# Seven products of quarters in place of the last expert's second product

## The chip, the core and the metric

The program runs on one core of a Trainium2 chip. The metric is the time of one execution on the device, in microseconds (us). The engines are TensorE (PE; PEld is its weight load), VectorE (DVE), ScalarE (ACT), GpSimd (POOL) and SyncE (SP), which here issues the transfers (DMAs).

## What is computed

Three layers follow one another, in float32: attention with a forgetting bias (2 x 8 heads, 576 tokens each), then a mixture of 8 experts on the 1152 tokens, then a bilinear layer.

```python
P = np.exp(logits)                 # then 8 rounds of row and column normalisation
for e in range(8):
    h = np.maximum(x @ w1[e], 0.0)         # 1152 x 512 by 512 x 1024: the first product
    ye = h @ w2[e]                         # 1152 x 1024 by 1024 x 512: the second product
    out += P[:, e:e + 1] * ye
a = out @ w_a
b = out @ w_b                              # 512 x 1536 each
return (a * b) @ w_out                     # 1536 x 512
```

## The kernel before

**Number format.** Every operand is split into a high and a low float16 half. A float32 product is three matmuls: high by high, high by low, low by high. A split is two instructions: ScalarE rounds the value to the high half (a plain copy that casts, or `hi_of`, L295, with a scale), and VectorE writes value minus high (`lo_of`, L309, for weights and for the last tokens; plain subtractions elsewhere).

**Tiles.** The 1152 tokens are 9 tiles of 128, in the order of the list `ORDER`. `xt` holds their transposed inputs, `ht` the hidden values (8 row blocks of 128 by 1152 tokens, two halves), `acc` the weighted sum over the experts. PSUM has eight banks, `mb0` to `mb2` and `yb0` to `yb4`.

**Stages.** Expert 0 runs beside the attention. Expert 1 makes its first product plainly (`h_plain`). Experts 2 to 7 make theirs by a Winograd form (`h_seven`): both operands are cut into quarters (tokens in two halves of 576, so `CN` is 288 columns) and seven products of quarters, each 6 matmuls of 288 columns, replace eight. Partial sums stay in PSUM; `dve_add` (L1713) and `act_copy` (L1717) move them between banks, and `out` (L1708, L1709) applies the maximum with zero and splits the result into `ht`. The sums of the inputs are made once (`x_sums`, L1622, tile `sx`), those of the weights for each expert (`w_sums`, L1656). The second product is plain in every expert: `y_tile` runs 24 matmuls of 512 columns for each tile (`y_part`, L1308 to L1310), and L1754 adds the scaled result to `acc`. In the last expert `xm_split` scales, splits and transposes each finished tile back into `xt`, and `x2_sums` (L1799) forms the sums that the bilinear layer's own seven products need. In that layer `ab_plain` (L1886) handles one tile plainly, `ab_seven` (L1924) eight tiles; `out_stage` (L2014) has matmuls of 256 columns.

**Conversions.** The bilinear layer's weights arrive as pairs of 32-bit words of float64 and are turned into float16 halves by `m2_prep`, 18 pieces, each a chain of some 16 VectorE instructions (L1525 to L1533, L1549, two of L309), a few on ScalarE and one on GpSimd. `m2_out` stores each piece in DRAM, and `m2_in` fetches it again. `M2N` says how many pairs of pieces each of the experts 1 to 7 carries beside its matmuls: none, then 4, 2, 4, 2, 4 and 2 pieces in experts 2 to 7. A piece may begin only after its expert's first product has written its first result (the key `hold`).

**Order.** Up to the first expert the order is written out by hand. From there on a planner (`Graph.schedule`) lays out all operations: each has an engine, or a choice between two, a cost in ns, the keys that it reads and writes, and a rank. The planner always takes the operation that can start first, and by rank among those within 60 ns. The result is a fixed order for each engine, and each engine runs its own list in order.

## Time and profile before

| what | us |
|---|---|
| median of 3 runs | 1011.77 (1010.45 to 1011.91) |
| the profiled execution, its own time | 1010.49 |
| its span, first to last instruction | 1008.8 |

The granted clock of TensorE is 1.0 of full speed (2.4 GHz) throughout. The profile is of one execution. Its span leaves out 1.7 us ahead of the first and behind the last instruction. A window is a stretch of the span; a group is all instructions with the same line, engine and operands. A busy TensorE is not one at its peak, since a matmul's record (0.38 us for 512 columns) overlaps those of its neighbours; the distance between starts, or a stretch divided by its count, tells more.

### The profile page before, as it was taken

The page shows a single profiled execution, that of the slowest core. Times are in us where ns is not written, and L with a number is a line of the kernel's source. Part 1 is how long each engine was busy: PE and PEld are TensorE (multiplying, and loading weights), DVE is VectorE, ACT ScalarE, POOL GpSimd, SP SyncE. Part 2 cuts the span into 40 slices and gives each one's busy share as a digit, 9 for nine tenths or more (in the row PEclk, how much of TensorE's full clock was granted, in tenths as well). Part 3 has the DMA queues.
Part 4 walks back from the last instruction along what each step waited for, and adds up shares of the span by engine and source line. Part 5 has one row for each costly group of instructions (what it writes and reads, how often), then busy time and mean ns, then how long its engine had stood idle before and what let it go on. Part 6 is the DMA issues. An engine that isn't in the chain of part 4 may idle for free.

```text
span 1008.8 us, 18859 instructions
## 1 busy us (share of the span) xinstructions
PE 989.8 (98%) x7534; PEld 629.5 (62%) x7534; DVE 774.8 (77%) x1661; ACT 530.9 (53%) x1009; POOL 99.7 (10%) x150
## 2 busy tenths in 40 slices
PE   6799999999999999999999999999999999999998
PEld 5677767665467547646744764674476464555777
DVE  4899996689858998875898896689888886667402
ACT  5798753563356438626644762663464454545220
POOL 3364563000000000000000000000000000000000
PEclk9999999999999999999999999999999999999999
DMA  9986999320241254224125414313446432313202
GB/s 235 208 167 123 172 168 171 97 94 1 76 134 43 84 209 167 84 97 154 44 104 188 167 69 137 130 43 116 177 171 244 97 85 84 126 44 124 84 21 74
DMA packets 152008, 121.38 MB, mean 120 GB/s; under 512 B 113360, under 2 KB 127696, under 8 KB 147312
## 3 DMA queue, kind: packets, MB, share of 16 engines
q1 hardware_dynamic: 147008, 117.78, 41.1%
q10 hardware_dynamic: 4912, 2.40, 1.0%
q8 instruction: 59, 0.97, 0.4%
q14 instruction: 29, 0.24, 0.1%
HBM read 79.26 MB, written 21.23 MB: 100 GB/s over the span
## 4 chain that ended last, share of the span: by engine, by line
PE 91%; DVE 3%; DMA 2%; ACT 1%; SPq 1%; issue 1%; POOL 1%; ACTq 0%; DVEq 0%; POOLq 0%
PE yb L1310 11%; PE yb L1309 11%; PE yb L1308 11%; PE yb L1700 4%; PE yb L1698 4%; PE yb L1699 4%; PE mb L1698 3%; PE mb L1699 3%; PE mb L1700 3%; PE yb L1925 2%; PE yb L1924 2%; PE yb L1926 2%; PE mb L1265 2%; PE mb L1267 2%; PE mb L1266 2%; PE mb L1925 2%
## 5 line engine op out<-in xcount | busy, mean ns | idle before, releaser
L1308 PE MATMUL yb<-wun,ht 128*128 128x512 f16 x504 | 191.0, 379 | 0.0
L1309 PE MATMUL yb<-wun,ht 128*128 128x512 f16 x504 | 191.0, 379 | 0.0
L1310 PE MATMUL yb<-wun,ht 128*128 128x512 f16 x504 | 191.0, 379 | 0.0
L1310 PEld LDWEIGHTS <-ht 128*128 128x128 f16 x504 | 49.3, 98 | 59.5
L1308 PEld LDWEIGHTS <-ht 128*128 128x128 f16 x504 | 49.4, 98 | 58.8
L1309 PEld LDWEIGHTS <-ht 128*128 128x128 f16 x504 | 49.3, 98 | 58.8
L1698 PE MATMUL yb<-sx,wun 128*128 128x288 f16 x288 | 82.4, 286 | 0.0
L1699 PE MATMUL yb<-sx,wun 128*128 128x288 f16 x288 | 82.4, 286 | 0.0
L1700 PE MATMUL yb<-sx,wun 128*128 128x288 f16 x288 | 82.4, 286 | 0.0
L309 DVE SCALAR_TENSOR_TENSOR wun<-stage,sc,wun 128x1024 f16<-128x1024 f32 (+1 forms) x70 | 75.9, 1108 | 7.7 <-ACT wun L295 7.5
L1754 DVE SCALAR_TENSOR_TENSOR acc<-yb,pe,acc 128x512 f32<-128x512 f32 x63 | 47.3, 750 | 44.5 <-PE yb L1310 43.6
L1699 PEld LDWEIGHTS <-wun 128*128 128x128 f16 x672 | 65.8, 98 | 17.5 <-issue 0.3
L1698 PEld LDWEIGHTS <-wun 128*128 128x128 f16 x672 | 65.8, 98 | 17.1
L1700 PEld LDWEIGHTS <-wun 128*128 128x128 f16 x672 | 65.8, 98 | 16.6
L295 ACT ACTIVATE wun<-stage,sc 128x1024 f16<-128x1024 f32 (+1 forms) x60 | 60.8, 1045 | 21.1 <-PE yb L1310 14.3
L292 ACT ACTIVATE jk<-stage 128x1024 f16<-128x1024 f32 x52 | 54.8, 1054 | 31.6 <-DMA stage<-in_moe_w_dram 30.9
L295 ACT ACTIVATE wun<-h,sc 128x1024 f16<-128x1024 f32 x36 | 41.1, 1144 | 27.1 <-issue 17.3
L1698 PE MATMUL mb<-xt,wun 128*128 128x288 f16 x192 | 54.9, 286 | 0.2 <-ACT yb L1717 0.2
L1700 PE MATMUL mb<-xt,wun 128*128 128x288 f16 x192 | 54.9, 286 | 0.0
L1699 PE MATMUL mb<-xt,wun 128*128 128x288 f16 x192 | 54.9, 286 | 0.0
L1708 ACT ACTIVATE ht<-yb 128x288 f16<-128x288 f32 x96 | 38.9, 408 | 26.5 <-PE yb L1700 26.3
L1288 PE MATMUL mb<-xt,wun 128*128 128x128 f16 x288 | 51.4, 222 | 0.6 <-DVE acc L1333 0.6
(507 smaller groups left out, 2553.4 us busy)
## 6 DMA issues: line engine op xcount, KB each, us to landing
stage<-in_moe_w_dram SPq DMA_DIRECT2D x26, 1024.0 KB, 5.1
md<-wun SPq DMA_DIRECT2D x18, 1024.0 KB, 3.9
wun<-md SPq DMA_DIRECT2D x12, 1024.0 KB, 4.8
mr<-in_moe_w_a_dram SPq DMA_DIRECT2D x12, 512.0 KB, 6.1
mr<-in_moe_w_b_dram SPq DMA_DIRECT2D x12, 512.0 KB, 3.5
mr<-in_moe_w_out_dram SPq DMA_DIRECT2D x12, 512.0 KB, 4.6
stage<-md SPq DMA_DIRECT2D x5, 1024.0 KB, 4.7
stage<-in_moe_w_dram SPq DMA_DIRECT2D x19, 256.0 KB, 4.1
```

What stands on the lines that cost most here:

```text
L292: nc.scalar.activation(out, src, AF.Square, accum_out=dst)
L295: nc.scalar.activation(hi, src, AF.Copy, scale=scale)
L309: eng.scalar_tensor_tensor(out=lo, in0=src, scalar=scale, in1=hi, op0=ALU.mult, op1=ALU.subtract)
L1288: nc.tensor.matmul(p, lhsT=wh, rhs=xh, start=(c == 0), stop=False)
L1308: nc.tensor.matmul(pp, lhsT=hh, rhs=wh, start=(f == 0), stop=False)
L1309: nc.tensor.matmul(pp, lhsT=hh, rhs=wl, start=False, stop=False)
L1310: nc.tensor.matmul(pp, lhsT=hl, rhs=wh, start=False, stop=(f == KF - 1))
L1698: nc.tensor.matmul(p, lhsT=wh, rhs=xh, start=first and ch == 0, stop=False, skip_group_check=True)
L1699: nc.tensor.matmul(p, lhsT=wh, rhs=xl, start=False, stop=False, skip_group_check=True)
L1700: nc.tensor.matmul(p, lhsT=wl, rhs=xh, start=False, stop=ch == 1, skip_group_check=True)
L1754: g.add("DVE", 663, lambda t=t, z=z: nc.vector.scalar_tensor_tensor(out=acc[:, t], in0=yb[z], scalar=pe[:, t, e:e + 1], in1=acc[:, t], op0 ...
L1925: nc.tensor.matmul(p, lhsT=wh, rhs=xl, start=False, stop=False, skip_group_check=True)
```

## The change

For the last expert (`YSEVEN`) the second product of eight of the nine tiles is made by seven products of quarters (`y_seven`): the 1024 hidden rows and the 512 output columns are halved, and the tokens are taken in pairs of tiles (`ORDER[kk]` and `ORDER[5 + kk]`). Matmuls have 256 columns. The ninth tile, `ORDER[4]`, is made plainly from four blocks (`rest_mm`), with 256 columns too.

The hidden values of that expert are no longer split by `out`. ScalarE writes them, scaled by 0.25, as float32 into `r`, a larger tile in the place of `ts0` and `ts1`. `h_parts`, called after each of the four rounds of `h_seven`, splits the quarters and forms their sums: four sums of 128x512 on GpSimd, eight low halves on VectorE, eight high halves on ScalarE, four of which may go to GpSimd. `w2_sums` forms and splits seven weight quarters: 4 subtractions, 7 high and 7 low halves of 128x1024, where `w_prep` had 4 and 4. The results lie in the new tile `wx`, in `units` 2 and 3 and in `sx`.

So that the quarters are whole tiles, `ORDER[4]` is divided between the two halves. `x_sums` reads `xt` through two pieces, and `x_turn` then moves the second half of `xt` by four transfers. In experts 2 to 6 the ninth tile's hidden values now lie in two places, and `r_copy` collects them into `wx` by two transfers per expert (256 KB each, pieces of 128 bytes); `y_tile` reads there for tile 4. `x2_sums` may put its sums on GpSimd for three of four groups. `M2N` gives experts 2 to 7 now 4, 4, 4, 4, 2 and 0 pieces.

```diff
+        big["wx"] = bp.tile([128, 2, 2, 1024], F16, name="wx")
         for i in range(2):
-            big["ts", i] = bp.tile([128, 1024], F32, name=f"ts{i}")
+            big["ts", i] = big["r"][:, i * 1024:(i + 1) * 1024]
...
+        def f():
+            nc.vector.tensor_scalar(pe[:, :, e], pe[:, :, e], inv1[e], inv2[e], op0=ALU.mult, op1=ALU.mult)
+            if e in YSEVEN:
+                nc.vector.tensor_scalar(pe[:, :, e], pe[:, :, e], 1.0 / HSC, None, op0=ALU.mult)
...
+            def X(z, r, t, c=c):
+                v = lambda c0, c1: xt[:, z, 2 * r + c, c0:c1]
+                return (lambda: (v(640, 1152), v(512 + 64, 640))) if t else (lambda: v(0, HT))
+
...
+    def x_turn():
+
+        rk = 203
+        xk = [("xt", t) for t in range(NTL)]
+        m = lambda: stage[2].bitcast(F16).rearrange("p (a t) -> p a t", a=8)
+        v = lambda c0, c1: xt[:, :, :, c0:c1].rearrange("p z c t -> p (z c) t")
+        n = lambda: h0[1].rearrange("p z f t -> p (z f t)")[:, 0:512].rearrange("p (a t) -> p a t", a=8)
+        mk = [("st", 2, c) for c in range(4)]
+        g.add("SP", 900, lambda: nc.sync.dma_start(out=m(), in_=v(640, 1152)), r=xk, w=mk, rank=rk)
+        g.add("SP", 200, lambda: nc.sync.dma_start(out=n(), in_=v(HT, 640)), r=xk, w=h0k[1], rank=rk)
+        g.add("SP", 900, lambda: nc.sync.dma_start(out=v(HT, 1088), in_=m()), r=mk, w=xk, rank=rk)
+        g.add("SP", 200, lambda: nc.sync.dma_start(out=v(1088, 1152), in_=n()), r=h0k[1], w=xk, rank=rk)
...
+    def h_parts(j):
+
+        R = lambda q: big["r"][:, q * HT:q * HT + 512]
+        k = lambda q: [("r", q, c) for c in range(2)]
+        rest = lambda: big["r"].rearrange("p (a b t) -> p a b t", a=2, b=2)[:, :, :, 512:HT]
+        home = lambda z: h_rest(z).rearrange("p (a f) (b t) -> p a f b t", a=2, b=2)[:, :, j]
+        rk = -4.5
+        g.add("ACT", 360, lambda: nc.scalar.activation(home(0), rest(), AF.Copy), r=rkeys, w=[("HR", 0, j)], rank=rk)
+        g.add("DVE", 420, lambda: nc.vector.tensor_tensor(out=home(1), in0=rest(), in1=home(0), op=ALU.subtract), r=rkeys + [("HR", 0, j)], w=[("HR", 1, j)], rank=rk)
+
+        def split(i, q, pool):
+            hi, lo = (lambda z=z: h_op(i, z)[:, j] for z in range(2))
+            g.add(("ACT", "POOL"), (620, 700), (lambda: nc.scalar.activation(hi(), R(q), AF.Copy), lambda: nc.gpsimd.tensor_copy(hi(), R(q))),
+                  r=k(q), w=[("H", i, 0, j)], rank=rk)
+            g.add("DVE", 690, lambda: nc.vector.tensor_tensor(out=lo(), in0=R(q), in1=hi(), op=ALU.subtract), r=k(q) + [("H", i, 0, j)], w=[("H", i, 1, j)], rank=rk)
+
+        def tt(o, a, b, op):
+            g.add("POOL", 1300, lambda: nc.gpsimd.tensor_tensor(out=R(o), in0=R(a), in1=R(b), op=op), r=k(a) + k(b), w=k(o), rank=rk)
+
+        split(1, 0, False)
+        split(2, 2, False)
+        split(4, 3, False)
+        tt(3, 1, 3, ALU.add)
+        split(5, 3, True)
+        tt(1, 0, 1, ALU.subtract)
+        split(7, 1, True)
+        tt(0, 3, 0, ALU.subtract)
+        split(6, 0, True)
+        tt(2, 2, 0, ALU.subtract)
+        split(3, 2, True)
...
+            v = [(lambda z=z: w2_at(e, i)(z)) for z in range(2)]
+            wk = w2_keys(e, i)
+            g.add("ACT", 1144, lambda: hi_of(v[0](), src(), sx), r=keys + [("ws", 2, e)], w=wk[0], rank=rank)
+            g.add("DVE", 1290, lambda: lo_of(nc.vector, v[1](), src(), sx, v[0]()), r=keys + [("ws", 2, e)] + wk[0], w=wk[1], rank=rank)
+
+        split(0, b11, k11)
+        sub(b11, b12, b11, k12, k11)
+        sub(b12, b22, b12, k22, k12)
+        split(3, b11, k11)
+        sub(b11, b22, b11, k22, k11)
+        split(4, b12, k12)
+        split(5, b11, k11)
+        split(1, b21, k21)
+        sub(b11, b21, b11, k21, k11)
+        split(2, b22, k22)
+        split(6, b11, k11)
...
+    def y_seven(e, hook):
+
+        wof = {1: 0, 2: 1, 3: 2, 4: 6, 5: 3, 6: 5, 7: 4}
+        G, gk = [lambda: yb[1], lambda: mb[0]], [[("yG", n, h) for h in range(2)] for n in range(2)]
+        Y, yk = [lambda: mb[2], lambda: mb[1]], [[("yY", n)] for n in range(2)]
+        links = [([("yb", 1)], gk[0]), (mbk(2), yk[0]), (mbk(0), gk[1]), (mbk(1), yk[1])]
...
+        def prod(i, kk, bank, bk, first, more=()):
+            wv, wk = w2_at(e, wof[i]), w2_keys(e, wof[i])
+            for j in range(4):
+                def mm(j=j):
+                    p = bank()
+                    hh, hl = (h_op(i, z)[:, j, kk * 128:(kk + 1) * 128] for z in range(2))
+                    wh, wl = (wv(z)[:, j] for z in range(2))
+                    nc.tensor.matmul(p, lhsT=hh, rhs=wh, start=first and j == 0, stop=False, skip_group_check=True)
+                    nc.tensor.matmul(p, lhsT=hh, rhs=wl, start=False, stop=False, skip_group_check=True)
+                    nc.tensor.matmul(p, lhsT=hl, rhs=wh, start=False, stop=j == 3, skip_group_check=True)
+
+                g.add("PE", 3 * 108, mm, r=[("H", i, z, j) for z in range(2)] + wk[0] + wk[1], w=bk + (list(more) if j == 0 else []), rank=frank())
+
+        def add(t, h, bank, bk, n=256):
+            v = lambda: acc[:, t, h * 256:h * 256 + n]
+            g.add("DVE", 440 if n == 256 else 750, lambda: nc.vector.scalar_tensor_tensor(
+                out=v(), in0=bank(), scalar=pe[:, t, e:e + 1], in1=v(), op0=ALU.mult, op1=ALU.add), r=bk + [("pe", e)], w=[("acc", t)], rank=-5)
+            g.add("-", LAG, lambda: None, w=bk)
+
+        half = lambda f, h: (lambda: f()[:, h * 256:(h + 1) * 256])
+        rest = []
+        for kk in range(5):
+            n = kk % 2
+            ta, tb = (ORDER[kk], ORDER[5 + kk]) if kk < 4 else (0, 0)
+            X, F, U = half(G[n], 0), half(G[n], 1), half(Y[n], 0)
+            xk, fk, uk = gk[n][0:1], gk[n][1:2], yk[n]
+            if kk < 4:
+                prod(1, kk, X, xk, True, fk)
+                prod(5, kk, F, fk, False)
+                g.add("ACT", 390, lambda U=U, X=X: nc.scalar.activation(U(), X(), AF.Copy), r=xk, w=uk, rank=-6)
+                g.add("-", LAG, lambda: None, w=xk + uk)
+                add(tb, 1, F, fk)
+                prod(2, kk, X, xk, False)
+                add(ta, 0, X, xk)
+            for f in rest:
+                f()
+            rest = []
+            if kk < 4:
+                prod(6, kk, U, uk, False)
+                add(ta, 1, U, uk)
+                prod(3, kk, F, fk, False)
+                add(ta, 1, F, fk)
+                prod(7, kk, U, uk, False)
+                add(tb, 1, U, uk)
+
+                def end(kk=kk, U=U, uk=uk, ta=ta, tb=tb):
+                    prod(4, kk, U, uk, False)
+                    add(tb, 0, U, uk)
+                    hook(ta)
+                    hook(tb)
+                    if kk:
+                        x2_sums(kk - 1)
+
+                rest.append(end)
...
+        def rest_mm(kh, wi, h, first):
+            wv, wk = w2_at(e, wi), w2_keys(e, wi)
+
+            def mm():
+                p = yb[0][:, h * 256:(h + 1) * 256]
+                for j in range(4):
+                    hh, hl = (h_rest(z)[:, 4 * kh + j] for z in range(2))
+                    wh, wl = (wv(z)[:, j] for z in range(2))
+                    nc.tensor.matmul(p, lhsT=hh, rhs=wh, start=first and j == 0, stop=False, skip_group_check=True)
+                    nc.tensor.matmul(p, lhsT=hh, rhs=wl, start=False, stop=False, skip_group_check=True)
+                    nc.tensor.matmul(p, lhsT=hl, rhs=wh, start=False, stop=j == 3, skip_group_check=True)
...
+        rest_mm(0, 0, 0, True)
+        add(t, 1, half(lambda: yb[0], 0), [("yb", 0)])
+        rest_mm(1, 2, 1, False)
+        rest_mm(0, 3, 1, False)
+        rest_mm(1, 1, 0, False)
+        add(t, 0, lambda: yb[0], [("yb", 0)], 512)
+        hook(t)
+        x2_sums(3)
...
+        seven = e in YSEVEN
+
         def out(src, bk, f, s_, c):
+            if seven:
+                q = 2 * (f // 4) + s_
+                g.add("ACT", 172 + CN / 1.2, lambda: nc.scalar.activation(big["r"][:, q * HT + c * CN:q * HT + (c + 1) * CN], src(), AF.Relu, scale=HSC),
+                      r=bk, w=[("r", q, c)], rank=-5)
+                return
...
+            if seven:
+                h_parts(j)
+
+    r_home = lambda: big["wx"].rearrange("p i z f -> p (i z f)")[:, 0:2048].rearrange("p (z f t) -> p z f t", z=2, f=8)
+
+    def r_copy():
+        for i, c0 in enumerate((512, 1088)):
+            g.add("SP", 400, lambda i=i, c0=c0: nc.sync.dma_start(
+                out=r_home()[:, :, :, i * 64:(i + 1) * 64].rearrange("p z f t -> p (z f) t"),
+                in_=big["ht"][:, :, :, c0:c0 + 64].rearrange("p z f t -> p (z f) t")),
+                r=[x for z in range(2) for f in range(KF) for x in hk(z, f, c0, c0 + 64)], w=[("wx", 0, y) for y in range(2)], rank=-4)
...
+        if e > 1 and p > 4:
+            dst, dkey = h_cols(p * 128 - 64, p * 128 + 64)
+        elif e > 1 and p == 4:
+            dst, dkey = (lambda z, f: r_home()[:, z, f]), (lambda z, f: [("wx", 0, y) for y in range(2)])
...
+            both = YSEVEN and not lo and kk < 3
+            g.add(("DVE", "POOL") if both else "DVE", (400, 750) if both else 400, tuple(fn) if both else fn[0], r=r, w=w, rank=rk)
...
-M2N = (0, 2, 1, 2, 1, 2, 1)
+M2N = (0, 2, 2, 2, 2, 1, 0)
+YSEVEN = (7,)
+HSC = 0.25
```

## Rows read from the trace of the kernel before

**Rows 1.** Page: the span, and busy time and share of each engine.

```profile
span 1008.8 us, 18859 instructions
...
PE 989.8 (98%) x7534; PEld 629.5 (62%) x7534; DVE 774.8 (77%) x1661; ACT 530.9 (53%) x1009; POOL 99.7 (10%) x150
```

**Rows 2.** Page, part 4: the chain that ended last, share of the span.

```profile
PE 91%; DVE 3%; DMA 2%; ACT 1%; SPq 1%; issue 1%; POOL 1%; ACTq 0%; DVEq 0%; POOLq 0%
```

**Rows 3.** Windows: stretch, its length, busy us (instructions) per engine, PEclk, DMA, GB/s.

```profile
379.40:466.46 87.06, 87.06 (x547) 53.42 (x546) 69.27 (x127) 48.30 (x86) 1.84 (x4) 1.00 0.31 109
466.46:554.24 87.78, 87.78 (x553) 54.01 (x552) 76.89 (x145) 47.30 (x89) 2.33 (x6) 1.00 0.37 132
683.50:730.12 46.62, 46.62 (x219) 21.13 (x216) 42.42 (x70) 18.20 (x25) 1.62 (x4) 1.00 0.43 158
730.12:771.28 41.16, 41.16 (x338) 32.88 (x336) 34.45 (x70) 26.01 (x56) 0.61 (x1) 1.00 0.45 158
771.28:817.90 46.62, 46.62 (x219) 21.13 (x216) 40.55 (x122) 18.09 (x37) 0.57 (x1) 1.00 0.49 150
817.90:825.94 8.04, 8.04 (x146) 8.04 (x144) 7.22 (x23) 5.08 (x14) 0.00 (x0) 1.00 0.71 196
944.07:974.20 30.13, 30.13 (x278) 27.01 (x276) 8.94 (x15) 6.51 (x14) 0.00 (x0) 1.00 0.24 88
```

**Rows 4.** Waits of TensorE from 560 to 575 us.

```profile
PE mb L1698 <- ACT yb L1717: 0.2, 1, 0.2
```

**Rows 5.** Groups by form, VectorE, expert 4: line, operation, count, busy us, mean ns, idle before.

```profile
L309 DVE SCALAR_TENSOR_TENSOR wun<-stage,sc,wun 128x1024 f16<-128x1024 f32 x6 | 7.7, 1280 | 1.0 <-ACT wun L295 1.0
...
L1754 DVE SCALAR_TENSOR_TENSOR acc<-yb,pe,acc 128x512 f32<-128x512 f32 x9 | 6.8, 751 | 3.4 <-PE yb L1310 3.1
...
L1533 DVE SCALAR_TENSOR_TENSOR h<-h,h 128x1024 int32<-128x1024 int32 x4 | 4.9, 1215 | 0.0
L1713 DVE TENSOR_TENSOR yb<-yb,sw 128x288 f32<-128x288 f32 x8 | 3.7, 462 | 1.3 <-PE yb L1700 1.3
...
L1549 DVE TENSOR_TENSOR h<-h,h 128x256 f32<-128x256 f32 x8 | 3.3, 418 | 0.0
...
L1526 DVE TENSOR_SCALAR h<-h,clampi 128x1024 f32<-128x1024 f32 x4 | 3.2, 807 | 0.0
L1528 DVE TENSOR_SCALAR h<-h 128x1024 int32<-128x1024 int32 x4 | 2.8, 695 | 0.0
...
L1656 DVE TENSOR_TENSOR ts<-stage,ts 128x1024 f32<-128x1024 f32 x2 | 2.4, 1220 | 0.0
```

**Rows 6.** Groups by form, VectorE, 818 to 944 us.

```profile
L1941 DVE TENSOR_TENSOR ht<-h,ht 128x512 f16<-128x512 f32 x10 | 6.6, 683 | 0.0
```

**Rows 7.** Groups by form, GpSimd, 97 to 170 us.

```profile
L977 POOL TENSOR_TENSOR pt<-p,pt 128x512 f16<-128x512 f32 x14 | 16.2, 1158 | 7.1 <-DMA raw<-pt 2.1 <-ACT pt L974 2.1 <-DVE pt L973 1.6
L974 POOL CAST pt<-p 128x512 f16<-128x512 f32 x9 | 5.9, 656 | 8.6 <-ACT p L1035 7.0 <-issue 1.6
```

**Rows 8.** Timeline, GpSimd and VectorE: start, length, instruction.

```profile
69.77 1.90 POOL L915 TENSOR_TENSOR pt<-p,pt 128x512 f16<-128x512 f32 x1 [4.53 <-ACT pt L912]
...
69.97 0.68 DVE L914 TENSOR_TENSOR pt<-p,pt 128x512 f16<-128x512 f32 x1
...
156.36 1.16 POOL L977 TENSOR_TENSOR pt<-p,pt 128x512 f16<-128x512 f32 x1 [2.11 <-DMA raw<-pt]
...
156.89 1.17 DVE L976 TENSOR_TENSOR pt<-p,pt 128x512 f16<-128x512 f32 x1 [0.57 <-ACT pt L974]
```

**Rows 9.** Timeline, VectorE and TensorE inside the last first product.

```profile
746.57 0.46 DVE L1713 TENSOR_TENSOR yb<-yb,sw 128x288 f32<-128x288 f32 x1
...
747.76 0.29 PE L1698 MATMUL yb<-sx,wun 128*128 128x288 f16 x1
```

**Rows 10.** Page, part 6: DMA issues, count, size, us to landing.

```profile
wun<-md SPq DMA_DIRECT2D x12, 1024.0 KB, 4.8
...
stage<-in_moe_w_dram SPq DMA_DIRECT2D x19, 256.0 KB, 4.1
```

More of the change, by code (lines that the diff above doesn't have):

```diff
@@ new lines, in w2_sums, with sub, split @@
+    def w2_sums(e, rank):
+        z0, z1 = wst[2, e]
+        sx = ws[2, e]
+        qk = [("q2", z, h) for z in (z0, z1) for h in range(2)]
+        stk = [("st", z, c) for z in (z0, z1) for c in range(4)]
+        g.add("-", 0, lambda: None, w=qk + stk)
+        b11, b12, b21, b22 = ((lambda z=z, h=h: stage[z].rearrange("p (c f) -> p c f", c=4)[:, :, h * 256:(h + 1) * 256]) for z in (z0, z1) for h in range(2))
+        k11, k12, k21, k22 = ([x] for x in qk)
+        def sub(o, a, b, r, w):
+            g.add("DVE", 1280, lambda: nc.vector.tensor_tensor(out=o(), in0=a(), in1=b(), op=ALU.subtract), r=r, w=w, rank=rank)
+        def split(i, src, keys):
+            v = [(lambda z=z: w2_at(e, i)(z)) for z in range(2)]
[13 more added lines that the diff above has]
+        split(6, b11, k11)
+        g.add("-", 0, lambda: None, w=qk + stk)
@@ L2131, in forgetting_attention_moe_bilinear_kernel @@
         else:
+            if e in YSEVEN:
+                h_link()
+                r_link()
             h_seven(e)
-        w_prep(2, e, (2, 3), prank())()
+            if e in YSEVEN:
+                r_link()
+            else:
+                r_copy()
+        if e in YSEVEN:
+            w_prep(2, e, (None, None), prank())
+            w2_sums(e, prank())
+        else:
+            w_prep(2, e, (2, 3), prank())()
         if e == 1:
             x_sums()
+            x_turn()
         if not last:
```

81 lines of the change are left out of this document (63 added, 18 removed).

## The prediction

> **What bounds the kernel now.** I read the page first: TensorE is busy 98% of the span [rows 1], and the chain that ended last lies 91% on it [rows 2]. Since a busy TensorE can still run thinly, the windows come next: each matmul has one weight load, so a stretch divided by PEld's count is the distance between starts. In the last expert's second product 216 matmuls of 512 columns take 46.62 us, 215.8 ns each; in the output stage 276 matmuls of 256 columns take 30.13 us, 109.2 ns each [rows 3]. That is 512 and 256 columns at 2.4 GHz plus 2.5 ns: there is no room between them, and the granted clock is 1.00 in every row. The waits then say how much is lost: in a whole stretch of an expert's first product one wait of 0.2 us [rows 4]. So from the experts on the time is the sum of the matmuls, and whatever makes TensorE wait is added in full. VectorE is next: 76.89 of 87.78 us in an expert with four conversions, 69.27 of 87.06 with two [rows 3]. GpSimd hardly works there (0.6 to 2.3 us per stretch). TensorE has little patience with VectorE in `h_seven`: an addition that began at 746.57 ended at 747.03, and the next product that waits for VectorE began at 747.76 [rows 9]: 0.7 us later.
>
> **The change, part by part.** The sum is made against the profiled execution, 1010.49 us, 1.28 below the median of 1011.77; the result is moved up by that.
>
> *Matmuls.* Plain: 9 tiles x 24 = 216 of 512 columns, 46.62 us. New: 7 products x 4 pairs x 12 = 336 of 256 columns, and 48 for the ninth tile, 384 in all; at 109.2 ns 41.93 us. **Gain 4.69 us.** I take the row of 256 columns as it stands, since there too every matmul had its own weight load and the loads were hidden (27.01 of 30.13 us busy [rows 3]). The Trainium skill ("TensorE: Matmul & The Clock Gate", Back-to-back issue gap) speaks against the change: it gives 81 ns per matmul at 128 columns and 131 at 512 in a stream with weight loads, so by an estimate between the two some 98 at 256, and then 384 matmuls would cost 37.6 us against 28.3, 9.3 more. The rows (215.8 and 109.2) don't bear it out.
>
> *VectorE in the last first product (41.16 us).* It loses 32 low halves in `out` (0.46 each [rows 5]). It keeps 16 additions, 16 x 0.46 = 7.4. `w2_sums` brings 4 subtractions of 1.22 and 7 low halves of 1.28 [rows 5], 13.8, where `w_prep` had 4 x 1.28. `h_parts` brings per round 7 low halves of 0.68 [rows 6] and one of half the size, 0.42 (as L1549 [rows 5]): 5.2, three rounds inside the stretch, 15.6. Sum 36.8, less about 0.08 per instruction in which the next one already starts: 33. That fits by itself. The conversions that leave would have cost two pieces here.
>
> *GpSimd beside it.* Four sums per round at 1.16 [rows 7], 4.6; up to four copies at 0.66 instead of ScalarE's. Three rounds inside the stretch: 13.9. Here lies the question. Where both engines read two operands from SBUF, they don't overlap: GpSimd's subtraction at 69.77 took 1.90 instead of 1.16 while VectorE's of 0.68 ran, and VectorE's at 156.89 took 1.17 instead of 0.68 behind GpSimd's [rows 8]. The Trainium skill ("SBUF — State Buffer", Who interferes with whom) states it as a lock: the later one waits to the end of the other. The trace agrees: 0.74 and 0.49 us were lost. The planner has no such term. All low halves and subtractions read two such operands; the additions read one in PSUM. In the last three rounds (30.9 us) VectorE has 18 us, with up to 5 more that `w2_sums` leaves over, and GpSimd 13.9: one after the other 32 to 37, 1 to 6 over; but 5.5 us of additions can run beside GpSimd, and `w2_sums` can begin in the expert before, which loses two conversions. Bounds 0 and 6.2; I take **1.0**, nearer to the lower end, since GpSimd has nothing before the first round ends and VectorE does most of the weights then.
>
> *The seam between the products.* The fourth round's sums come after the last matmul of the first product. On GpSimd: 0.4 for the last maximum, 1.16 per sum, 0.6 and 0.68 for the halves, some 0.15 per hand-over, so the fifth product's operand is whole about 4 us behind the seam and the last one 7.5. TensorE has meanwhile the first and second product of two pairs (4 x 12 x 0.109 = 5.2) and three quarters of two others (3.9). Cover 9 against 7.5, but each sum may lose 0.74: 10.5. Bounds 0 and 3; I take **0.6**.
>
> *Rest of the second product.* 25 additions of 256 columns to `acc` (0.46 each, as the 288 of L1713) and a whole one take the place of 9 of 0.75 [rows 5], and each frees a bank that the next product but one needs, 1.3 us later. The conversions that are gone made room, and some of `x2_sums` goes to GpSimd. Bounds 0 and 2; I take **0.3**. The tail is as before: `ab_plain` (8.04 us [rows 3]) covers the last tile's transposition.
>
> *Conversions.* Experts 3 and 5 get two pieces more: per piece 3 x 0.69, 0.81, 2 x 1.22, 4 x 0.42, 2 x 1.28 and small ones [rows 5], about 10, so 20 on 69.27 less a few that the preceding expert no longer hands on: 84 of 87. Expert 4 had four pieces and lost 0.2 [rows 3, 4]. If `w_sums` is late, the next first product is. Bounds 0 and 2; I take **0.3**. It comes at lower rank than the additions that TensorE waits for, so it is the weights that slip, and they have half a stage in hand.
>
> *Transfers.* `r_copy` moves 2 x 256 KB per expert, from experts 2 to 6; 256 KB took 4.1 us, 1 MB 4.8 [rows 10]. It has four tiles, 4 x 5.18 = 20.7 us, before tile 4 reads it; pieces of 128 bytes may double that and it still fits. It also holds SP's queue for two issues, some 1 us, ahead of stores that wait for VectorE anyway. `x_turn`, four transfers, waits for `x_sums` in expert 1, a second product ahead of its reader. Cost 0 for both, hidden by those tiles; without that cover `r_copy` would cost its 2 x 4.1 = 8.2 us in an expert, `x_turn` its 4.8 twice.
>
> Sum: 1010.49 - 4.69 + 1.0 + 0.6 + 0.3 + 0.3 = 1008.0; with 1.28, **1009.3 us**.
>
> **Rivals.** (a) *Every cover holds*: the new waits cost under 1 us in all. For it: the lock's rows are few, and VectorE's own 33 us fit. Time 1011.77 - 4.69 = 1007.1 and up to 1008.0. (b) *The gain is taken back*: waits of 2.7 to 6.7 us at several of the places above. Time 1009.8 to 1013.8, no change that can be told. (c) *The lock decides*: in the last three rounds of the last first product GpSimd's 13.9 us and VectorE's 23 run strictly one after the other, and the fourth round's come behind the seam: 6.2 + 3 = 9.2 lost, 1011.77 - 4.69 + 9.2 = 1016.3, slower. It decides once VectorE is late by more than the 4.7 us that the matmuls give; against it stands that the additions need no second port, and that ScalarE (26.01 of 41.16 us [rows 3]) takes the high halves. The rule of the Trainium skill's SBUF page is this case. (d) *Narrow matmuls are not cheaper by half*: with a new operand each 109 ns some of the weight load stays uncovered. A load is 97.9 ns (27.01 us by 276 [rows 3]); a quarter of it in the open makes 133.7 ns, 51.3 us for the product, 4.7 more than before: 1016.5. The gain is gone at 121.4 ns (46.62 by 384). The 109.2 of the output stage speak against it. The Trainium skill's rule on gaps (above) is of this kind. (e) *The seven products are not made* or the order elsewhere changes so that nothing comes of it: the diff leaves no plain product in that expert, so this is nearly excluded.
>
> **How the numbers follow.** A measurement of this kernel can tell some 0.2%, 2.0 us, from no change. Chances: the forecast (waits of 1 to 2.7 us, 1008.1 to 1009.7) 0.30; (a) 0.25; (b) 0.26, with (e) 0.01 in "same"; (c) 0.15; (d) 0.01; and 0.02 for a queue order that makes a late load cost more than the gain. Faster 0.55, same 0.27, slower 0.18. The range begins at 1006.9 (every cover holds, and the 0.2 of the old wait goes too) and ends at 1015.0, inside (c), so that the most costly part of (c), (d) and the queue are left out, together with what may fall under (a). The likeliest sign's own range is 1006.9 to 1009.7.
>
> **What would show it.** Right: TensorE's starts 109 ns apart from the seam on, 384 matmuls, the second product 42 to 44 us long; GpSimd's sums at 1.2 to 1.9; the last first product 41.2 to 43 us long; no long wait at the start of the experts 3 to 6. Wrong: the last first product 45 us or more, with TensorE waiting for L1713's additions while VectorE's low halves last 1 us and more (c); a wait for `wx` or `xt` behind a transfer; starts farther apart than 115 ns without a wait (d).

## The result, and the profile after

The changed kernel takes 1024.72 us (median of 4 runs, 1024.12 to 1025.23) where the kernel before takes 1011.11 beside it: ratio 1.0138, 95% interval 1.0120 to 1.0155. It is slower by 13.6 us; the forecast was 1009.3, the range ended at 1015.0. The profiled execution spans 1023.0 us against 1008.8.

The page of the changed kernel: span, engines, and the chain that ended last [answering to rows 1 and 2].

```profile
span 1023.0 us, 19344 instructions
...
PE 989.9 (97%) x7702; PEld 647.3 (63%) x7702; DVE 797.3 (78%) x1664; ACT 544.3 (53%) x1036; POOL 159.6 (16%) x208
...
PE 81%; DVE 9%; DMA 5%; ACT 2%; POOL 2%; issue 1%; ACTq 0%; SPq 0%; DVEq 0%; POOLq 0%
```

The chain lay 91% on TensorE; it is 81% now, and VectorE has 9% of it. The windows of the changed kernel, by stage [rows 3]: expert 6's second product, the last first product (to the seam), the last second product, the start of the next stage, and a stretch inside the second of these.

```profile
684.45:731.80 47.35, 47.35 (x224) 21.74 (x222) 37.19 (x68) 18.59 (x23) 2.19 (x3) 1.00 0.38 122
731.80:784.47 52.67, 45.27 (x352) 35.01 (x351) 44.55 (x59) 31.34 (x68) 28.61 (x23) 0.97 0.09 32
784.47:830.23 45.76, 41.47 (x371) 35.97 (x369) 33.73 (x90) 19.53 (x44) 21.34 (x25) 1.00 0.43 143
830.23:838.30 8.07, 7.38 (x132) 7.25 (x130) 6.81 (x22) 5.64 (x17) 5.60 (x8) 1.00 0.64 196
752.14:761.00 8.86, 4.74 (x27) 3.16 (x26) 7.37 (x8) 5.30 (x13) 7.86 (x8) 0.81 0.01 2
```

The last first product has grown most. Its 52.67 us hold 42.82 us of matmuls at their undisturbed distances (15 of the second product's are already among them): 9.85 lost. The second product's 369 remaining matmuls need 40.32 of 45.76: 5.44 lost. Expert 6's first product has 1.75 us of waits that were not there, the next stage 1.75 (by starts). In sum 18.8 lost; less the 4.69 that the matmuls give, 14.1 of the 14.2 us between the spans. TensorE's waits from 640 to 845 us (what it waited for: us, times, longest):

```profile
PE yb L1916 <- DVE sw L1938: 5.4, 3, 4.1
PE yb L1916 <- DVE yb L1938: 2.0, 2, 1.5
PE yb L1823 <- DVE acc L1831: 1.4, 2, 0.8
PE mb L1823 <- ACT ts L1927: 1.2, 1, 1.2
PE mb L1916 <- ACT sw L1942: 0.9, 1, 0.9
...
PE mb L2166 <- DMA xt<-ts: 0.7, 1, 0.7
PE yb L2128 <- DVE acc L1831: 0.7, 1, 0.7
PE mb L1916 <- ACT yb L1942: 0.5, 1, 0.5
PE yb L1823 <- ACT mb L1845: 0.5, 1, 0.5
```

L1938 is the addition that stood on L1713 [rows 9]. What held it is in the timeline (start, length, instruction, idle before it), GpSimd, VectorE and TensorE put together:

```profile
742.04 2.29 POOL L1740 CAST ht<-ts 128x512 f16<-128x512 f32 x2 [8.14 <-ACT ts L1927]
...
748.12 0.92 DVE L1938 TENSOR_TENSOR yb<-yb,sw 128x288 f32<-128x288 f32 x2
...
751.03 5.94 POOL L1745 TENSOR_TENSOR ts<-ts 128x512 f32<-128x512 f32 x4 [6.70 <-issue]
...
752.98 1.19 DVE L1742 TENSOR_TENSOR ht<-ts,ht 128x512 f16<-128x512 f32 x1 [3.94 <-ACT ht L1740]
...
755.76 0.81 DVE L1938 TENSOR_TENSOR sw<-yb,sw 128x288 f32<-128x288 f32 x2
...
756.26 0.28 PE L1916 MATMUL yb<-xt,wun 128*128 128x288 f16 x1 [4.12 <-DVE sw L1938]
...
757.69 0.44 PE L1916 MATMUL yb<-xt,wun 128*128 128x288 f16 x1
```

GpSimd's first sum (L1745) began at 751.03, after 6.70 us for which the profile shows no releaser; the last of its operands' other readers had ended at 745.81. What the timeline leaves out, the instructions of GpSimd's sequencer, stands in the view by source line (the changed kernel, then the last such row of the kernel before):

```profile
L1745 POOLq MODIFY_POOL_CONFIG  x2: 7/7/7, 744.3 to 744.4; - x2
```

```profile
L457 POOLq MODIFY_POOL_CONFIG  x2: 11/11/11, 192.2 to 192.2; - x2
```

The pair at 744.3 lies right behind the two copies (CAST), 6.6 us ahead of the first sum. The kernel before has two such pairs, at 3.8 and 192.2, each followed by a wait of GpSimd for VectorE of 13.9 us or more that covers it, and none from there to its end.

VectorE's next low half waited for the high half of that sum, the additions stood behind it on VectorE, and TensorE behind them (4.12 us between the modelled end and the next start, 4.28 more than the usual distance by starts). Then the granted clock fell: 0.81 over that window, the last row a matmul at the lower level, 240 ns from start to start instead of 122, 1.74 us over 15 of them.

The groups by form in the last first product (VectorE, then GpSimd) [rows 5 to 7]:

```profile
L1742 DVE TENSOR_TENSOR ht<-ts,ht 128x512 f16<-128x512 f32 x12 | 10.2, 874 | 4.4 <-ACT ht L1740 3.9 <-POOL ht L1740 0.5
L309 DVE SCALAR_TENSOR_TENSOR wun<-stage,sc,wun 128x1024 f16<-128x1024 f32 x4 | 7.1, 1774 | 0.0
...
L1938 DVE TENSOR_TENSOR yb<-yb,sw 128x288 f32<-128x288 f32 x8 | 3.7, 458 | 1.2 <-ACT wx L295 1.2
...
L1745 POOL TENSOR_TENSOR ts<-ts 128x512 f32<-128x512 f32 x12 | 19.1, 1592 | 9.6 <-issue 6.7 <-DVE ht L1742 2.3
L1740 POOL CAST ht<-ts 128x512 f16<-128x512 f32 x8 | 7.9, 1004 | 12.6 <-ACT ts L1927 12.6
```

The low halves take 874 ns instead of 683, the scaled ones 1774 instead of 1280, while the additions that read PSUM keep their 0.46 us.

### The profile page after: what moved, and what is told of

Read it like the earlier page. It is cut to its first block, busy times and chain, and to the rows that moved or that the text cites. A ratio compares the mean times of both kernels' runs of the same rounds, so it can differ in the third digit from the quotient of the medians.

```text
span 1023.0 us, 19344 instructions
## 1 busy us (share of the span) xinstructions
PE 989.9 (97%) x7702; PEld 647.3 (63%) x7702; DVE 797.3 (78%) x1664; ACT 544.3 (53%) x1036; POOL 159.6 (16%) x208
## 4 chain that ended last, share of the span: by engine, by line
PE 81%; DVE 9%; DMA 5%; ACT 2%; POOL 2%; issue 1%; ACTq 0%; SPq 0%; DVEq 0%; POOLq 0%
PE yb L1310 8%; PE yb L1309 8%; PE yb L1308 8%; PE yb L1918 4%; PE yb L1917 4%; PE yb L1916 4%; DMA stage<-in_moe_w_dram 3%; PE mb L1916 3%; PE mb L1918 3%; PE mb L1917 3%; PE yb L2167 2%; PE yb L2168 2%; PE yb L2166 2%; DVE wun L309 2%; PE mb L1265 2%; PE mb L2166 2%
## 5 line engine op out<-in xcount | busy, mean ns | idle before, releaser
L1308 PE MATMUL yb<-wun,ht 128*128 128x512 f16 x392 | 148.6, 379 | 0.0
L1309 PE MATMUL yb<-wun,ht 128*128 128x512 f16 x392 | 148.6, 379 | 0.0
L1310 PE MATMUL yb<-wun,ht 128*128 128x512 f16 x392 | 148.6, 379 | 0.0
L292 ACT ACTIVATE jk<-stage 128x1024 f16<-128x1024 f32 x52 | 54.8, 1054 | 29.4 <-DMA stage<-in_moe_w_dram 28.7
L1310 PEld LDWEIGHTS <-ht 128*128 128x128 f16 x392 | 38.3, 98 | 46.2
L1308 PEld LDWEIGHTS <-ht 128*128 128x128 f16 x392 | 38.4, 98 | 45.6
L1309 PEld LDWEIGHTS <-ht 128*128 128x128 f16 x392 | 38.3, 98 | 45.6
L1994 DVE SCALAR_TENSOR_TENSOR acc<-yb,pe,acc 128x512 f32<-128x512 f32 x54 | 40.4, 749 | 30.8 <-PE yb L1310 30.5
L292 ACT ACTIVATE jk<-h 128x1024 f16<-128x1024 f32 x18 | 19.0, 1054 | 69.9 <-DVE h L1540 69.8
```

The costliest lines, as they stand in the source:

```text
L292: nc.scalar.activation(out, src, AF.Square, accum_out=dst)
L1308: nc.tensor.matmul(pp, lhsT=hh, rhs=wh, start=(f == 0), stop=False)
L1309: nc.tensor.matmul(pp, lhsT=hh, rhs=wl, start=False, stop=False)
L1310: nc.tensor.matmul(pp, lhsT=hl, rhs=wh, start=False, stop=(f == KF - 1))
L1994: g.add("DVE", 663, lambda t=t, z=z: nc.vector.scalar_tensor_tensor(out=acc[:, t], in0=yb[z], scalar=pe[:, t, e:e + 1], in1=acc[:, t], op0 ...
```

## The experiments

Time is the median of the runs; behind it stands the ratio to the kernel before, run beside it. Edits are against the changed kernel unless another is named.

### The late first sum

**e1_preload.** One GpSimd addition of a single column, ahead of everything else of GpSimd's for w2(7).

```
+ g.add("POOL", 6000, lambda: nc.gpsimd.tensor_tensor(out=lib, in0=ws[2, E - 1], in1=ws[2, E - 1], op=ALU.add), r=[("ws", 2, e)], w=["lib"], rank=-20)
  w2_sums(e, prank())
```

> One GpSimd addition of a single column is put ahead of everything else that GpSimd does for the last expert's second-product weights, behind the scale of w2(7) (known at about 735 us); nothing waits for it. Theory A (GpSimd pays about 5 us before the first addition after the all-reduces, with no operand missing, and this is what held the low half, VectorE's eviction additions behind it and then TensorE for 4.28 us at 752 us, after which the granted clock fell): the idle stretch of over 5 us now lies before the one-column addition, the first sum of the weights starts within 1 us of its last operand, the 4.28 us wait and the half-rate matmuls at 757 to 761 us go, and the span falls by 4 to 6.5 us against the changed kernel, to 1016.5 to 1019 us. Theory B (the wait comes of the exclusion of VectorE by GpSimd alone): the sums start where they did, the span stays within 1 us of the changed kernel's 1023.0. Theory C (VectorE simply has too much to do in this stretch): TensorE waits as long in all, at other places; span within 2 us of 1023.0.

Measured: 1022.59 us, 1.0115 (1.0100 to 1.0131); span 1019.7, 3.3 less. GpSimd's timeline:

```profile
733.58 0.35 POOL L457 PARTITION_ALL_REDUCE sc<-sc  x1 [23.69 <-DVE sc L450]
741.24 0.18 POOL L2385 TENSOR_TENSOR sc<-sc 128x1 f32<-128x1 f32 x1 [7.30 <-DVE sw L1938]
742.20 2.31 POOL L1740 CAST ht<-ts 128x512 f16<-128x512 f32 x2 [0.78 <-ACT ts L1927]
746.14 4.38 POOL L1745 TENSOR_TENSOR ts<-ts 128x512 f32<-128x512 f32 x2 [1.63 <-ACT yb L1942]
```

The delay went where the column is: it reads a scale known at 734.7 and began 6.5 us later, and the sums began at 746.14. (The releaser named in the row is only the last event before it.) The pair moved with it:

```profile
L2385 POOLq MODIFY_POOL_CONFIG  x2: 83/83/83, 733.9 to 733.9; - x2
```

So the delay belongs to the change from GpSimd's all-reduces to its additions, not to an operand; the copies (CAST) at 742 in the changed kernel, behind an all-reduce and ahead of the pair, had not paid it. The Trainium skill ("GPSIMD Engine Reference", Instruction dispatch) says that the first call of a newly loaded kernel pays about 6 us of loading that shows as no instruction of its own. The 6.6 and 7.2 us from the pair to the next instruction agree in size, though here the sequencer's pair marks the place. The 4.28 us wait is gone, but not its whole price: waits of 2.37 us at 761.6 and 0.3 to 0.6 at five places came up, with the lower clock again behind the largest (0.57 of full speed from 764.5 to 768.5). A half-hit: theory A's place, but 3.3 us instead of its 4 to 6.5. Something else holds VectorE too: it is busy 44.98 of that stage's 49.41 us.

**e8_m2n.** On e1_preload: `M2N = (0, 2, 2, 2, 1, 2, 0)` for `(0, 2, 2, 2, 2, 1, 0)`.

> On top of e1_preload, experts 5 and 6 carry one and two portions of the conversions instead of two and one (expert 6 then as many as in the kernel before). Theory that the 1.66 us of waits in expert 6's first product (at 645 and 677 us) come from its buffers still being busy with expert 5's second portion: they go, and the span is 1.2 to 1.8 us below e1_preload's 1019.7. Rival (the place where the last portion ends decides): the waits move into expert 6's second product or the last expert's start, the span is within 0.6 us of 1019.7 or above.

Measured: 1032.95 us, 1.0225 (1.0204 to 1.0245); span 1031.0. Expert 6's waits went, as expected, and 20 us came up in the last first product. This order puts an all-reduce of the conversions behind the column, and GpSimd pays both ways:

```profile
738.55 0.50 POOL L2385 TENSOR_TENSOR sc<-sc 128x1 f32<-128x1 f32 x1 [7.17 <-DVE sw L1938]
744.78 0.38 POOL L1546 PARTITION_ALL_REDUCE sc<-sc  x1 [5.74 <-issue]
...
759.91 2.16 POOL L1745 TENSOR_TENSOR ts<-ts 128x512 f32<-128x512 f32 x1 [13.64 <-DVE ht L1742]
```

and by source line:

```profile
L1546 POOLq MODIFY_POOL_CONFIG  x2: 7/7/7, 739.2 to 739.3; - x2
```

Neither theory had this in view. It confirms the delay, with its pair, on the way back too (the sum at 759.91 has a third pair, at 746.2, hidden by its wait for VectorE), and leaves the conversions to e15_m2n.

### Who holds VectorE

**e2_dve_sums.** The operand's sums to VectorE (`"POOL", 1300, ... nc.gpsimd` becomes `"DVE", 690, ... nc.vector`), high halves on ScalarE alone, `both = False` in `x2_sums`.

> All sums of the last expert's w2 quarters and of its operand quarters go to VectorE, the high halves to ScalarE alone, so that GpSimd does nothing beside VectorE in the last first product and the second. VectorE takes on some 30 operations, about 18 to 20 us by 0.62 to 0.69 us each. Lock theory (VectorE is held out by GpSimd's additions and conversions): the low halves are back at 0.66 to 0.70 us, the evictions of the last first product at 1.28 us, and the stalls of the second product of 5.44 us fall to under 2; span 1012 to 1017 us. Library theory alone (only the wait at 752 us goes): the stalls of the second product stay at 4 to 5.5 us; 1016.5 to 1019. Rival (VectorE is overfull, whoever holds it): the last first product is 45 us or longer again and the span is 1020 us or more.

Measured: 1030.31 us, 1.0196 (1.0175 to 1.0217). The lock theory's time did not come; the rival's did (first product 46.86 us, span 1028.6). VectorE's operations are back at 0.68, but it runs without a gap from 751.6 to 761.6, and ScalarE's copies of accumulators into `r` (L1927) wait until VectorE has summed and split what lies there. TensorE loses 3.9 us in the last first product, 10.8 in the second and 8.3 behind it. So GpSimd's help is needed; the question is its price.

**e5_acthigh.** On e1_preload, high halves on ScalarE alone (`g.add("ACT", 620, ...)` for `("ACT", "POOL")`).

> On top of e1_preload (span 1019.7) the high halves of the operand quarters are made on ScalarE alone; GpSimd keeps the sums only. In e1_preload ten of these conversions stood on GpSimd in the last first product, 0.98 us each in the mean (0.61 alone), and VectorE's low halves took 0.96 us (0.68 alone). Lock theory: VectorE wins back a part of what the exclusion takes, 1.5 to 4 us of span: 1015.7 to 1018.2. Rival (the long part is the chain sum, high half, low half, and ScalarE's place in it): ScalarE, with 35 us of work in that stretch, delays its copies of the accumulators, and the span is 1019.5 or more.

Measured: 1025.40 us, 1.0138 (1.0111 to 1.0164). The rival's time holds, in three of four executions (1025.3 to 1025.6; the fourth took 1020.53). TensorE waits 3.5 us for L1927, which waits for low halves of the round before and stands behind high halves on ScalarE, and nothing is won.

**e6_nosums and e7_idle.** On e5_acthigh; e7 keeps 16 additions, into a tile that nobody reads.

```
e6:  def tt(o, a, b, op):
+        return
...
e7:  g.add("POOL", 1300, lambda: nc.gpsimd.tensor_tensor(out=big["idle"], in0=big["idle"], in1=big["idle"], op=op), r=[("HR", 0, j)], w=["idle"], rank=rk)
```

> As e5_acthigh, but the 16 sums of the operand's quarters are left out (the halves are made from quarters that were not summed, so the second product's operands are not the right ones); VectorE and ScalarE do all that they did. GpSimd then does nothing in the last first product. Lock or chain theory: the last first product is back at 41.2 to 43 us with low halves of 0.66 to 0.70 us, and the seam's waits of 1.33, 0.99 and 0.41 us shrink; span 1008 to 1012. Rival (VectorE has too much to do even undisturbed): its work at undisturbed prices is 20 x 0.68 + 7 x 1.28 + 16 x 0.45 + 4 x 1.22 + 2.6 = 37.2 us of 41.2, too near to full; the last first product is over 45 us and the span over 1014.

> As e6_nosums, but GpSimd does 16 additions of the same size (128x512, 32 bits) into a tile of its own, four behind each piece of the rest's high half; no engine waits for them and they keep no buffer. Lock theory: they alone lengthen VectorE's operations (low halves 0.9 us or more in the mean beside them, 1.28 us evictions up to 2), and the span is 3 to 8 us over e6_nosums. Rival (chain theory: the sums cost because low halves wait for them, not because VectorE is held out): the span is within 1 us of e6_nosums.

Measured: e6 1019.23 us, 1.0083 (1.0060 to 1.0107), span 1014.2; e7 1026.55 us, 1.0163 (1.0145 to 1.0181), span 1023.9. e6's profiled execution took 1015.93 us and its others 1018.84 to 1020.53; where those lost more is in no trace. Windows over the last first product (columns as above), e6 and e7:

```profile
731.00:771.30 40.30, 40.30 (x331) 32.19 (x330) 31.49 (x58) 35.26 (x79) 0.55 (x2) 1.00 0.08 27
```

```profile
731.00:780.00 49.00, 42.86 (x334) 33.05 (x333) 42.86 (x58) 34.99 (x80) 25.00 (x18) 0.97 0.07 23
```

The same 58 VectorE instructions take 31.49 us without and 42.86 with additions that no engine waits for (nothing held them, so they ran back to back, from 740.4 to 765.7). Groups of e6, then of e7:

```profile
L1742 DVE TENSOR_TENSOR ht<-ts,ht 128x512 f16<-128x512 f32 x16 | 10.7, 684 | 2.6 <-ACT ht L1740 2.6
```

```profile
L1746 DVE TENSOR_TENSOR ht<-ts,ht 128x512 f16<-128x512 f32 x13 | 12.6, 985 | 0.5 <-ACT ht L1744 0.5
...
L1749 POOL TENSOR_TENSOR idle<-idle 128x512 f32<-128x512 f32 x16 | 24.1, 1508 | 1.2
```

This is the exclusion of [rows 8], by itself: 11.4 us of VectorE for 24 of GpSimd, and 8.3 us lost by TensorE in the first product, lower clock included (nothing in e6, whose 40.30 us are all matmuls). The chain rival falls. The lock theory's 3 to 8 us are met at the medians (7.3) and passed by the spans (9.7). e6's own span misses its 1008 to 1012: 4.0 us are lost in the second product, 5.1 behind it and 1.3 in expert 6.

**e14_before_idle.** On e4_conversions (below; second product as before the change): the column and 16 such additions.

```
+ for _ in range(16):
+     g.add("POOL", 1300, lambda: nc.gpsimd.tensor_tensor(out=big["idle"], in0=big["idle"], in1=big["idle"], op=ALU.add), w=["idle"], rank=-20)
```

> As e4_conversions (second product as before the change, no conversions in the last expert), plus 16 GpSimd additions of 128x512 into a tile of their own in the last first product, behind a one-column addition that starts them at about 741 us; nobody waits for them. VectorE there has about 33 us of work in 41.2 without the conversions. Theory that the exclusion alone is what costs, whatever VectorE's own list: they take 20 to 26 us back to back, VectorE's evictions of 0.45 us beside them stay (they read PSUM) while its SBUF operations of 1.28 us become 1.6 to 2.3; with some 8 us of slack in VectorE's list and only 7 such operations exposed, 0 to 4 us over e4_conversions (span 1010.1 to 1014). Rival (the forecast's case that the lock decides, 9.2 us whatever else is there): 1017 us of span or more.

Measured: 1013.53 us, 1.0028 (1.0017 to 1.0038), one us over e4_conversions. Windows of the last first product, e4_conversions and then e14_before_idle:

```profile
731.45:772.61 41.16, 41.16 (x337) 32.87 (x336) 25.34 (x59) 23.79 (x55) 0.35 (x1) 1.00 0.23 81
```

```profile
732.72:774.86 42.14, 41.32 (x337) 32.87 (x336) 28.69 (x59) 23.54 (x55) 20.09 (x18) 1.00 0.23 81
```

Here VectorE reads PSUM in 40 of its 59 operations and has 16 us free: 3.35 us of it are taken, and 0.98 reach TensorE. Six of VectorE's operations beside these additions read SBUF alone, 17 did in e7: 0.56 and 0.67 us of VectorE for each. So GpSimd's additions are not dear in themselves; by these two runs the count of such operations sets what VectorE loses, and its free time how much of that TensorE sees.

**e10_costs.** On e9_fbank (below), the planner's durations as in contention (sums 1750, low halves 960, scaled ones 1800).

> As e9_fbank, with the durations that the order of work is planned with set to what the trace shows in contention: GpSimd's sums 1750 ns instead of 1300, the low halves of the operand 960 instead of 690, the scaled low halves of w2(7) 1800 instead of 1290. No instruction is added. Theory that a good part of the last first product's 6.10 us of waits comes of an order planned for undisturbed durations: 1.5 to 4 us below e9_fbank. Rival (VectorE's work with the exclusion, 49.4 us against 40.5 us of matmuls, sets the length, in whatever order): within 1.5 us of e9_fbank, either way.

Measured: 1026.49 us, 1.0166 (1.0149 to 1.0183), 7.8 over e9_fbank: a miss for both. The new order loses 11.8 us in the last first product instead of 6.1, 4.4 of them in waits for ScalarE's copies into `r` (L1927, here L1928), and nothing from the seam on instead of 2.6. What it shows is how much one order differs from another here; it settles no cause.

### The second product's own waits

The timeline of the changed kernel, one pair of tiles (TensorE, ScalarE, VectorE put together):

```profile
805.48 0.27 PE L1825 MATMUL yb<-wx,ht 128*128 128x256 f16 x1
...
805.78 0.37 ACT L1845 ACTIVATE mb<-yb 128x256 f32<-128x256 f32 x1
...
806.20 0.27 PE L1823 MATMUL yb<-wx,ht 128*128 128x256 f16 x1 [0.46 <-ACT mb L1845]
...
807.40 0.27 PE L1825 MATMUL yb<-wun,ht 128*128 128x256 f16 x1
...
807.71 0.48 DVE L1831 SCALAR_TENSOR_TENSOR acc<-yb,pe,acc 128x256 f32<-128x256 f32 x1 [0.85 <-PE yb L1825]
...
808.25 0.27 PE L1823 MATMUL yb<-wun,ht 128*128 128x256 f16 x1 [0.58 <-DVE acc L1831]
```

The copy out of the lower half of a bank starts when the last matmul queued into the upper half ends, and the next matmul into that bank starts when the copy is done; the addition out of the upper half likewise: 0.62 and 0.74 us. All four are waits on semaphores, so it is the program's own synchronisation that takes the bank as one; what the chip would do without it is in no run.

**e9_fbank, e12_fbank_flags, e13_fbank_full.** On e1_preload, products 5 and 3 in banks of their own; e12 and e13 add a matmul into the columns above 255 at each one's last use. As e9 and e12 ran, the next stage's accumulators in those two banks lack a term in columns that the first matmul there had marked for overwriting and nothing had written; e13 writes all of them.

```
- X, F, U = half(G[n], 0), half(G[n], 1), half(Y[n], 0)
+ X, F, U = half(G[n], 0), half(lambda n=n: yb[2 + n], 0), half(Y[n], 0)
...
- prod(1, kk, X, xk, True, fk)
- prod(5, kk, F, fk, False)
+ prod(1, kk, X, xk, True)
+ prod(5, kk, F, fk, True)
...
e13: + nc.tensor.matmul(flags()[:, 256:512], lhsT=hl, rhs=wh, start=False, stop=False, skip_group_check=True)
```

> On top of e1_preload, the accumulators of products 5 and 3 of the second product get a PSUM bank of their own (two banks that the first product has left), instead of the upper half of the bank in whose lower half products 1 and 2 are summed. Theory (each copy or addition out of one half waits for the last matmul queued into the other half, and the next matmul into that bank waits for the copy or addition in turn: 0.62 and 0.74 us for every pair of token tiles, whatever else runs): these waits go, the second product's stalls fall from 5.45 us to 1 to 2.5 us (the seam's stay), span 1015.3 to 1017.5 against 1019.7. Rival (the copy or addition comes late because ScalarE and VectorE are busy with the splits of the next stage): the waits stay within 1 us in the sum, span 1019 or more.

> As e9_fbank, with two matmuls of 32 columns (one at the end of the last product 3 in each of the two new banks) that write columns 256 to 287 of those banks, which e9_fbank had marked for overwriting by its first matmul and never written, so that the next stage's first accumulation there replaced what it should have added to. Theory: time as e9_fbank within 1.5 us (span 1015.5 to 1018.5, ratio to the kernel before 1.006 to 1.0105), the second product's stalls 1.5 to 2.5 us. Rival for the cause of the 0.62 and 0.74 us waits (they went in e9_fbank by chance of another order): they are back here. It stays slower than the kernel before, since the exclusion in the last first product (6.7 us of waits), the late weights of expert 6 (1.65) and the late sums behind (1.7) are more than the 4.69 us gained.

> As e12_fbank_flags, but the two extra matmuls write columns 256 to 511 of the new banks, which is as wide as the next stage accumulates there. Theory: the next stage's accumulators add up again, and the time is as e9_fbank within 1.5 us (ratio to the kernel before 1.006 to 1.0105), the second product's stalls 1.5 to 2.5 us. Rival: the shared banks' waits come back with this order, and it is 1019.7 us of span or more.

Measured: e9 1018.72 us, 1.0087 (1.0072 to 1.0102); e12 1018.98, 1.0084 (1.0070 to 1.0099); e13 1019.28, 1.0093 (1.0078 to 1.0108), its second product:

```profile
780.57:823.73 43.16, 41.84 (x378) 36.63 (x378) 34.73 (x90) 19.24 (x44) 21.69 (x24) 1.00 0.45 151
```

The waits are gone in all three: 1.97, 1.99 and 1.96 us of stalls instead of 5.45, what is left lying at the seam. The shared bank cost 3.5 us: 2.72 in the four waits of 0.62 and 0.74, the rest at the seam. Of the kernels that leave nothing out, e13 is the fastest with seven products: 5.4 us faster than the change, and still 0.9% behind the kernel before, which no version with seven products beats. Its profiled execution loses 6.8 us up to the seam, 2.0 behind it in the second product, 1.7 in expert 6 and 2.0 in the next stage; no version that leaves nothing out is without such losses.

**e11_nosums_fbank.** e6_nosums with these banks, and no GpSimd in the next stage's sums.

> As e6_nosums (the 16 sums of the operand's quarters left out, high halves on ScalarE), with the banks of e9_fbank, and the sums for the stage behind all on VectorE, so that GpSimd does nothing beside VectorE from 735 us to the end of that stage. Theory that exclusion, library and shared banks are all that took the matmul gain away, beside the conversions: last first product 41 to 42 us, second product 42 to 43.5 us (45.6 in e6_nosums), span 1005.5 to 1009, below the kernel before by up to 3 us. Rival (something else in the second product costs too): second product 44.5 us or more, span over 1010.

Measured: 1016.54 us, 1.0067 (1.0048 to 1.0086), span 1014.4. Both products ran without a wait, 41.2 and 41.9 us of matmuls: the gain of 4.69 is there in full. Time still was not won, since the next thing is late, in the first `ab_seven`:

```profile
PE mb L2167 <- ACT acc L2046: 5.3, 1, 5.3
```

That is the sums for the stage behind (`x2_sums`), done by VectorE alone after the second product; with two shorter waits and the lower clock that followed, 8.5 us are lost there. The stages' part of the theory holds, its time doesn't.

### What the moves cost by themselves

**e3_layout, e4_conversions, e15_m2n.** `YSEVEN = ()` in all three, and `M2N` as before the change, as the change has it, and `(0, 2, 2, 2, 1, 2, 0)`.

> The second product of the last expert is computed as before the change, and the conversions of the mixture weights are shared among the experts as before; what is left is the change of layout that the seven products need (the transposed operand's copies and transfers and the order of the rest). Theory that the layout costs nothing, as the stages of experts 1 to 5 show: within 1 us of the kernel before (1011.1 us). Theory that a part of the loss comes from the layout: 2 us or more above it.

> The second product of the last expert is computed as before the change, but the conversions of the mixture weights are shared among the experts as the change has it (none in the last expert, more in experts 3 and 5). Theory that the move is nearly free: 0 to 1 us above the run without it (e3_layout). Theory that the crowding of experts 5 and 6 costs: the 1.7 us of waits at 645 and 677 us appear here too, and the time is 1.5 to 2.5 us above e3_layout. A gain is possible as well, since the last expert is freed of conversions: up to 1 us below.

> As e4_conversions, but experts 5 and 6 carry one and two portions of the conversions instead of two and one; the last expert none. Theory that expert 6's waits come from expert 5's second portion, which keeps the buffers of expert 6's weights so that ScalarE stands before weights that have not landed, with its copies of accumulators queued behind: the waits go and the time is that of e3_layout (1011.1) within 0.7 us. Rival (the weights of the last expert come later instead): the waits appear in the last first product, and the time is that of e4_conversions (1012.6) or more.

Measured: e3 1011.11 us, 1.0004 (0.9994 to 1.0013); e4 1012.58, 1.0015 (1.0005 to 1.0024); e15 1010.90, 1.0008 (0.9997 to 1.0018). The layout is free. In e4 ScalarE waits in expert 6's first product for weights that have not landed:

```profile
ACT jk L292 <- DMA stage<-in_moe_w_dram: 5.8, 2, 3.6
```

No such wait stands in e3 or e15. Behind L292 on ScalarE stand the copies of accumulators, and TensorE waits 1.46 us for them, as much as e4 took over e3. The last expert can lose its conversions for nothing if expert 5 keeps one portion. Which buffer or queue delayed the load was not followed up. The delay varies: in e12's profiled execution, 1022.58 us where its others took 1017.8 to 1019.3, it cost 5.40 us.

## Why the prediction was wrong

**Matmuls: right.** 4.69 us by 109.2 ns; the starts are 109 ns apart wherever nothing is waited for (805.48 and its neighbours), and e11 has the gain whole. Rival (d) is out. The gap that the Trainium skill gives for streams with weight loads ("TensorE: Matmul & The Clock Gate", Back-to-back issue gap), which spoke against the change, is not what the trace shows.

**"GpSimd beside it", 1.0 with bounds 0 and 6.2: 9.85 measured.** This is the step that failed, in three ways. The delay ahead of the first addition was not in the sum at all: GpSimd started 5.2 us after its operand was ready, and TensorE had a wait of 4.28 and 1.74 of low clock behind it. e1 gave back 3.3 of these 6.0, since other waits came up in their place. The rows shown before could not tell of it, as that part of the kernel had only all-reduces on GpSimd. Second, the exclusion was priced near its lower bound, with "VectorE does most of the weights then" as the reason, and with two lists that were too short. VectorE's was 3 us longer than the 33 of the forecast: 31.5 in e6, with four pieces of w2 (4.7 us) still to come behind the seam. GpSimd's was put at 13.9 for the sums alone; the copies were named but not added, and with ten of them it was busy for 28.6. In e7 sixteen additions alone lengthened VectorE's list by 11.4 us. The Trainium skill ("SBUF — State Buffer", Who interferes with whom) states a lock between the two engines. e7's low halves, 985 ns beside the additions instead of 684, agree with that. Third, 5.5 us of additions that "can run beside GpSimd" don't help when they stand on VectorE's queue behind a held operation.

**The seam, 0.6 (0 to 3).** Waits of 0.63 (also in the 9.85) and 1.32 us on either side of it, then 0.98 and 0.40: 3.3, above the upper bound. The third ended with the bank, but with banks of its own e9 keeps 0.83 of it, for a low half.

**Rest of the second product, 0.3 (0 to 2).** "Each frees a bank that the next product but one needs" was the wrong reading: two accumulators share a bank, and the next matmul needs it at once. 2.72 us in the later pairs, 3.5 with what the seam gained, shown by e9 and e13.

**Conversions, 0.3 (0 to 2): 1.75.** The mechanism was as told (the weights slip); that they have half a stage in hand was not so, and it was ScalarE's queue, not VectorE's, that carried the delay to TensorE.

**The tail, "as before": 1.75.** An addition (0.86) and a transposition (0.89) came late; `ab_plain` did not cover them. No run took these up by themselves. **Transfers, 0:** right, by e3.

Rival (c) had the largest cause and the sign, and came to 1016.3 with 9.2 us; the first product alone took that. Its signs came too: 52.67 us, waits for L1713's additions (now L1938), low halves of 0.87 to 1.24 us. That 9.85 lies so near 9.2 is chance: 6.0 of it followed GpSimd's late start, which (c) did not have. The forecast treated (b) and (c) as alternatives, yet the small waits came beside the large one: 1.75 + 5.44 + 1.75, 8.9 us more.

## What to carry to other kernels

When work goes to a free engine, price it on the neighbour that it shares memory with: beside a full VectorE that works on SBUF, GpSimd's 24 us took 11.4 of its time, beside one with slack and PSUM operands 20 us took 3.35. If an engine gets a kind of operation that it has not run in that phase, look for instructions of its sequencer by source line, let a tiny operation pay the delay early, and check that no older kind follows it. Two accumulators in one bank were one resource to this program, and several covers of half a microsecond are to be added up, not ranked.

## Not expected of the hardware

GpSimd's changes between all-reduces and additions took 5 to 7 us each, both ways (5.74 back to an all-reduce in e8), idle in the timeline, with a pair of MODIFY_POOL_CONFIG on its sequencer at the start of each. Behind some waits TensorE ran the next matmuls at the lower of its two levels: 14 of them behind 4.28 us in the changed kernel, which put 1.7 us on top, and as many in e9 behind 2.38 us and shorter waits before it; e6's wait of 3.08 us at 835 had no such tail. A matmul that opens an accumulation marks columns of its bank beyond those it writes: in e9 and e12 what the next stage added there replaced what it should have joined, until all 512 columns had been written (e13).
